# Attention and ELU feed-forward in one kernel: other loads, turns and setup in the first 70 microseconds

## The chip, the cores and the metric

The kernel runs on one core of a Trainium2 chip. The metric is the device time of one execution in microseconds (us). The engines are PE (TensorE, matmuls; PEld is its loading of weights), DVE (VectorE), ACT (ScalarE), POOL (GpSimd) and SP (SyncE, which here only issues DMAs). Each engine works through its own queue in order; waits between queues are semaphores. A DMA issue takes time on the engine that issues it.

## The reference

Causal attention with a window of 128 and a linear bias per head, for 8 batches, 8 heads, 576 positions and a head size of 64, and behind it a feed-forward layer with ELU:

```python
scores = scale * np.matmul(q, k.transpose(0, 1, 3, 2))
...
mask = (rel >= 0) & (rel < window)
scores = np.where(mask, scores + bias[None], -1000000000.0)
...
attn = np.exp(scores)
attn = attn / (np.sum(attn, axis=-1, keepdims=True) + 1e-09)
return np.matmul(attn, v).astype(np.float32)
...
h = x @ w_in
g = np.where(h > 0.0, h, alpha * (np.exp(np.minimum(h, 0.0)) - 1.0))
return (g @ w_out).astype(np.float32)
```

The 8 x 576 rows of x (512 wide) are the attention output of all heads; w_in is 512 x 2048, w_out 2048 x 512. Inputs and output are float32.

## The kernel before

All matmul operands are float16; the loads convert. A batch's positions are cut into 5 blocks (four of 128, one of 64). `BANKS` lists 16 score groups per batch: block 0 in two groups of four heads, blocks 1 to 3 in four groups of two heads, block 4 in two groups of four heads. For a group, `scores(b, s)` multiplies keys by queries into one PSUM bank (four to eight matmuls; for batch 0 four or two more with `cI` and `DM` that add bias and mask) and ACT takes the exponential into `EX`. `cut` (batch 1 on) masks by a minimum on DVE. `values(b, s)` multiplies `EX` by the values `VP`; a column of ones in `VP` gives the sums. `normalize(b, i, half)` divides on DVE (L424, L425) into `xn`; `turn(b, i)` transposes `xn` to `xT` (batches 0 and 1 on PE with a DVE copy, L438 and L440; later ones by a DMA).

The feed-forward part works on blocks t of 512 rows of x, 16 pieces j each. `hidden(t, j)` is 16 matmuls (8 wide ones from t = 2 on) of `w_in_sb` and `xT` into one of three `hp` banks (L461); ACT takes the exponential `e` (L465), POOL clamps it (L466). `elu(t, j)`, one step later, joins both on DVE into `g` (L473). `output(t, j)` is four matmuls of `g` with a quarter of `w_out_sb` (L504); after four of them ACT copies the bank to `ob` (L508) and SP writes it out. For t = 0 piece j uses rows 128*(j//4) on and the w_in columns 512*(j%4) on, so pieces 0 and 4 use the first chunk of `w_in`.

How q and k get to `QK`, heads on the free axis and the 64 head dimensions on partitions: batch 0 by `transposes_half(a, hq, w)`, eight PE transposes (L290) of half a of the positions, four heads, k (w = 1) or q (w = 0), with four copies each (L296; k on ACT, q on DVE); batch 1 by `transposes` (`put` copies first on DVE, then on ACT, both L308); the last 64 positions by `transposes_tail` (L341, DVE copies L346); from batch 2 on by `squares` on DVE and `collect` DMAs. v is loaded into `vs` and copied into `VP` by `place_v`, each copy one set of 32 rows, on DVE (L123), ACT (L125) or POOL (L121).

PSUM has 8 banks: two for scores, transposes and turns (`ps_s`), two for value groups (`ps_v`, `av`), three for `hp` (`ps_h`), one for `op` (`ps_o`).

What runs when is written by hand. `at(s, f, ...)` puts a call into step s, `HID` and `OUT` say which piece of `hidden` and `output` a step holds, `LATER` delays them from given pieces on. A step is emitted in this order: scores; hidden; elu of the step before; `early` calls; `later` calls (values and normalize, then turns); everything else (copies of v, DMA issues, setup); output. Each engine's queue follows that order.

Batch 0 starts with `transposes_half` of the first half of the positions. `warm(n)` issues n idle matmuls of the identity (L536) in the first steps. All loads are issued by POOL, in its queue, between its other work. The setup that the masks of later batches need is done on DVE by `zeros` (L211 to L216), `groups` (L227), `terms` (L241), `last_blocks` (L201), `group_rows` (L252), `bands` (L208) and `k_term` (L270), by `fill_q` on ACT (L261) and `fill_k` on POOL (L265); `fill_other` copies the rows to the other `QK` by DMA.

The steps of before around the change, on PE:

- steps 0 to 4: scores(0, s), eight fillers, values of the group before, from step 4 with hidden(0,0), then hidden(0,1) in step 5;
- steps 6 and 7: values(0,5) and the four `transposes_half` of the second half, then turn(0,1);
- steps 8 to 17: scores(0, 6) to (0, 15), one hidden piece each, values; from step 13 outputs of t = 0;
- steps 18 to 21: the four `transposes` of batch 1; scores(1,0) in step 21.

Of the kernel before, what the change touches and what calls it, by code (L numbers as in the profile page):

```python
# [19 lines left out]
def kernel(  # L20
# [9 lines left out]
    nc = tc.nc  # L30
# [7 lines left out]
    XBAR = 2  # L38
    RING = 3 * S

    LATER = {16: (3, 4), 24: (4, 5), 30: (5, 5), 32: (6, 6), 40: (7, 7)}
    VW = D + 2
    V = nc.vector

# [4 lines left out]
    ps_s = ctx.enter_context(tc.tile_pool(name="ps_s", bufs=2, space=PSUM))  # L49
    ps_v = ctx.enter_context(tc.tile_pool(name="ps_v", bufs=2, space=PSUM))  # L50
    ps_h = ctx.enter_context(tc.tile_pool(name="ps_h", bufs=3, space=PSUM))
    ps_o = ctx.enter_context(tc.tile_pool(name="ps_o", bufs=1, space=PSUM))
# [33 lines left out]
    def load_half(b, w, a, h0=0, h1=H):  # L86
        if b not in stq:
            stq[b] = stage.tile([128, 2, H, 4, D], F16, name="stq")
        nc.gpsimd.dma_start(
            stq[b][64 * a:64 * a + 64, w, h0:h1, :, :].rearrange("p h j d -> p h (j d)"),  # L90
            (q, k)[w][b, h0:h1, 256 * a:256 * a + 256, :].rearrange("h (p j) d -> p h (j d)", j=4))

    def load_v_half(b, a):
        if b not in vs:
            vs[b] = stage.tile([128, H, 4, D], F16, name="vs", tag="vs", bufs=2)
        nc.gpsimd.dma_start(
            vs[b][64 * a:64 * a + 64, :, :, :].rearrange("p h j d -> p h (j d)"),
            v[b, :, 256 * a:256 * a + 256, :].rearrange("h (p j) d -> p h (j d)", j=4))
# [28 lines left out]
    def load_wi(i, n=1):  # L127
        c = slice(512 * i, 512 * i + 512 * n)
        nc.gpsimd.dma_start(w_in_sb[:, :, c], moe_w_in[:, c].rearrange("(c p) f -> p c f", p=128))
# [8 lines left out]
    with tc.manual_schedule():  # L138
# [9 lines left out]
        load_half(0, 0, 0, 4, 8)  # L148
        load_v_half(0, 0)
        load_wi(0)  # L150
        load_wi(1)
        load_half(0, 1, 1)
        load_half(0, 0, 1)
        nc.gpsimd.iota(posi[:, 0:512].rearrange("p (n j i) -> p n j i", j=4, i=32),
                       pattern=[[128, 4], [1, 4], [4, 32]], base=0, channel_multiplier=0)
        nc.gpsimd.iota(posi[:, 512:576], pattern=[[1, 64]], base=512, channel_multiplier=0)
# [295 lines left out]
        def hidden(t, j):  # L452
            w, c0, f0, nf = place(t, j)
            p = hps[t, j] = ps_h.tile([128, 512], F32, name="hp", tag="hp")
            a = (512 * t + c0) % RING
            cuts = [(0, w, a)] if a + w <= RING else [(0, RING - a, a), (RING - a, w, 0)]
            for l in range(nf):
                fc = f0 + l
                for u0, u1, x0 in cuts:
                    for c in range(4):  # L460
                        nc.tensor.matmul(  # L461
                            p[:, l * w + u0:l * w + u1], w_in_sb[:, c, fc * 128:(fc + 1) * 128],
                            xT[:, c, x0:x0 + u1 - u0], start=(c == 0), stop=(c == 3))
            e = es[t, j] = work.tile([128, 512], F32, name="e", tag="e")
            nc.scalar.activation(e, p, AF.Exp)  # L465
            nc.gpsimd.tensor_scalar(out=e, in0=e, scalar1=1.0, scalar2=0.0, op0=ALU.min, op1=ALU.max)  # L466
# [66 lines left out]
        def warm(n):  # L533

            for _ in range(n):
                nc.tensor.matmul(spare[:, 0:128], ident, ident, start=True, stop=True)  # L536
# [4 lines left out]
        def at(s, f, *a):  # L541
            tasks.setdefault(s, []).append((f, a))


        HID, OUT, late = {}, {}, (0, 0)
        first = [0, 1, 4, 5, 2, 6, 3, 7]
        for m in range(16 * NTB):
            late = LATER.get(m, late)
            t, j = divmod(m, 16)
            HID[m + (4 if m < 2 else 6) + late[0]] = t, first[m] if m < 8 else j  # L550
            OUT[13 + m + late[1]] = t, j
        warm(20)
        transposes_half(0, 0, 1, ps_h, "hp")
        warm(8)
# [6 lines left out]
        at(0, place_v, 0, 0, (2,), nc.scalar)  # L561
        at(0, place_v, 0, 0, (3,), nc.gpsimd)
        at(0, place_v, 0, 1, (0, 1, 2), nc.gpsimd)
        at(0, load_v_half, 0, 1)
        at(0, load_wi, 2)
        at(1, scores, 0, 1)
        at(1, warm, 8)
        at(1, place_v, 0, 1, (3,), nc.scalar)
        for i in (2, 3, 4):
            at(i, warm, 8)  # L570

        for b in range(B):
            s0 = 16 * b + (5 if b else 2)
            for s in range(16):
                i, p = BANKS[s]
                half = p if i in (0, 4) else p // 2
                sv = s if b == 0 and s < 6 else s0 + s
                if b or s > 1:
                    at(sv, scores, b, s)
                if b:  # L580
                    at(sv, cut, b, s)
                sv += 2 if b > 2 or b == 2 and s > 1 else 1
                at(sv, values, b, s)
                if i in (0, 4) or p % 2:
                    at(sv, normalize, b, i, half)
                    if half:
                        at(sv + 1, turn, b, i)
            if b == 0:
                for hq in range(2):
                    at(6 + hq, transposes_half, 1, hq, 1, *((ps_h, "hp") if hq else (ps_o, "op")))  # L590
                    at(6 + hq, transposes_half, 1, hq, 0, *((ps_h, "hp") if hq else (ps_s, "sps")))
                at(14, transposes_tail, 0)
            if b + 1 < B:
                for hp in range(NP if b == 0 else 0):
                    at(18 + hp, transposes, 1, hp)
                for n in range(8 if b else 0):
                    at(s0 + (2 + n if b > 1 else (1, 2, 5, 6, 3, 4, 7, 12)[n]), squares, b + 1, n)
                    at(s0 + (6 + n if b > 1 else 8 + n if n < 4 else 9 + n), collect, b + 1, n)
                at(s0 + (24 if b else 31), transposes_tail, b + 1)
            if b + 2 < B and b:  # L600
                for i, w in enumerate((1, 0)):
                    at(s0 + 10 + 3 * i, load_qk, b + 2, w)
                    at(s0 + 26 + i, load_tail, b + 2, w)
                at(s0 + 15, load_v4, b + 2)
                at(s0 + 19, load_v4_tail, b + 2)
                for n in range(4):
                    for u in range(2):
                        at(s0 + 20 + 2 * n + u, place_v, b + 2, n, (2 * u, 2 * u + 1), nc.gpsimd)


        for u in range(2):
            at(6 + u, place_v, 0, 2, (2 * u, 2 * u + 1), nc.gpsimd)
            at(10 + u, place_v, 0, 3, (2 * u, 2 * u + 1), nc.gpsimd)
        at(1, load_wi, 3)
        at(3, load_wo, 0, 1)
        at(8, terms)
        at(5, load_wo, 1, 1)
        at(8, load_wo, 2, 1)
        at(10, load_wo, 3, 1)
        at(3, zeros)  # L620
        at(8, last_blocks)
        at(5, groups)
        at(10, group_rows)
        at(12, bands)
        for n, m in enumerate((12, 15, 18, 23, 26)):
            at(m, fill_q, n)
            at(m, fill_k, n)
        for h in range(H):
            at(12 + h, k_term, h)
        for n in range(5):  # L630
            at((21, 22, 23, 25, 28)[n], fill_other, n)
        for i, w in enumerate((1, 0)):
            at(6 + i, load_tail, 0, w)
            at(12 + i, load_qk, 1, w)
            at(17 + i, load_qk, 2, w)
            at(16 + 5 * i, load_tail, 1, w)
            at(38 + i, load_tail, 2, w)
        at(8, load_v4_tail, 0)
        at(14, load_v4, 1)
        at(22, load_v4_tail, 1)  # L640
        at(20, place_v, 1, 0, (0, 1), V)
        at(21, place_v, 1, 0, (2, 3), V)
# [9 lines left out]

        for s in range(max(OUT) + 1):
            now = tasks.get(s, [])
            early = [x for x in now if x[0] in (cut, transposes_half, transposes, transposes_tail, warm)]
            later = [x for x in now if x[0] in (values, normalize)] + [x for x in now if x[0] is turn]
            for f, a in now:
                if f is scores:
                    f(*a)
            if s in HID:  # L660
                hidden(*HID[s])
            if s - 1 in HID:
                elu(*HID[s - 1])
            for f, a in early + later:
                f(*a)
            for x in now:
                if x not in early and x not in later and x[0] is not scores:
                    x[0](*x[1])
            if s in OUT:
                output(*OUT[s])  # L670
# [30 lines left out]
```

## Time and profile before

| what | value |
|---|---|
| median of five runs | 348.54 us (345.94 to 349.95) |
| the profiled execution, one of the five | 349.95 us |
| its span, first to last instruction | 348.2 us |
| PE busy | 329.1 us, 95% |
| DVE, POOL, ACT busy | 250.1, 213.8, 207.6 us |
| mean granted clock of PE | 0.988 |
| read from and written to memory | 36.70 and 9.44 MB |

The busy shares are averages over the whole span. PE's time holds 143.1 us of output matmuls (L504), 152.2 us of hidden matmuls (L461), 51.0 us of scores (L358) and 7.7 us of the 68 fillers (L536). Where a line of a timeline has square brackets, they hold the engine's idle time before that line and what ended it. In lists of waits the columns are total us, times, longest. In the clock row of the page each digit is one fortieth of the span, in tenths of full speed.

### The profile page before, as it was taken

What the parts mean: (1) busy time and instruction counts of PE and PEld (TensorE: products, weight loads), DVE (VectorE), ACT (ScalarE), POOL (GpSimd) and SP (SyncE); (2) the same over time, 40 slices, a digit from 0 to 9 for tenths busy, and PEclk for the clock granted to TensorE, in tenths of its full rate; (3) what the DMA queues carried; (4) which work ended last, traced back from release to release, by engine and by line L of the source; (5) the groups of instructions that cost most, each with busy time, mean ns of one, the idle gap of its engine ahead of it and who ended that gap; (6) DMA issues with size and microseconds to landing.
All of it is one profiled execution on the core that took longest, in us unless ns stands there. A gap on an engine that the chain in (4) does not pass through costs nothing.

```text
span 348.2 us, 9296 instructions
## 1 busy us (share of the span) xinstructions
PE 329.1 (95%) x3588; PEld 244.1 (70%) x3588; DVE 250.1 (72%) x572; ACT 207.6 (60%) x359; POOL 213.8 (61%) x326
## 2 busy tenths in 40 slices
PE   5979899798989989999999999999999999999995
PEld 4758677477766757777777777777777777766664
DVE  4587788889769679949994999498967676533330
ACT  5564657977875646665656665666566666344431
POOL 8655966654778955995689568947972223333330
PEclk9996999999999999999999999999999999999999
DMA  7999599956992698479968984996462222311122
GB/s 89 188 201 138 77 175 168 195 100 128 141 167 60 112 202 115 108 106 196 110 107 121 196 108 93 146 189 94 105 107 56 54 47 50 70 34 32 30 60 64
DMA packets 66428, 39.54 MB, mean 114 GB/s; under 512 B 31120, under 2 KB 60048, under 8 KB 66384
## 3 DMA queue, kind: packets, MB, share of 16 engines
q0 software_dynamic: 41936, 18.35, 44.6%
q1 hardware_dynamic: 24272, 20.46, 26.7%
q8 instruction: 28, 0.46, 0.5%
q10 hardware_dynamic: 176, 0.13, 0.1%
q14 instruction: 16, 0.13, 0.1%
HBM read 36.70 MB, written 9.44 MB: 133 GB/s over the span
## 4 chain that ended last, share of the span: by engine, by line
PE 79%; DVE 8%; DMA 5%; POOL 3%; ACT 2%; issue 1%; SPq 1%; POOLq 0%; DVEq 0%; ACTq 0%
PE hp L461 32%; PE op L504 30%; PE sp L358 7%; PE av L404 4%; DMA xT<-xn 2%; DMA QK<-tt 2%; PE spare L536 2%; DVE g L473 2%; DVE EX L390 2%; DVE tt L327 2%; PE sp L378 1%; POOL VP L121 1%; DVE xn L425 1%; POOL e L466 1%; ACT e L465 1%
## 5 line engine op out<-in xcount | busy, mean ns | idle before, releaser
L466 POOL TENSOR_SCALAR e<-e 128x512 f32<-128x512 f32 x144 | 90.4, 629 | 113.5 <-ACT e L465 103.7
L461 PE MATMUL hp<-xT,wi 128*128 128x256 f16 (+3 forms) x1536 | 152.2, 248 | 1.2 <-DVE xT L440 0.6
L473 DVE SCALAR_TENSOR_TENSOR g<-e,hp 128x512 f16<-128x512 f32 x144 | 98.0, 681 | 67.8 <-POOL e L466 66.8
L504 PE MATMUL op<-wo,g 128*128 128x512 f16 x560 | 143.1, 379 | 0.6 <-ACT ob L508 0.6
L461 PEld LDWEIGHTS <-wi 128*128 128x128 f16 x1536 | 119.6, 99 | 15.2 <-issue 1.1
L382 ACT ACTIVATE EX<-sp 128x512 f16<-128x512 f32 x128 | 76.6, 598 | 64.8 <-PE sp L358 50.9
L465 ACT ACTIVATE e<-hp 128x512 f32<-128x512 f32 x144 | 86.0, 597 | 48.5 <-PE hp L461 46.7
L121 POOL TENSOR_SCALAR VP<-vs 32x512 f16<-32x512 f16 x106 | 70.2, 662 | 8.7 <-DMA vs<-in_v_dram 1.6
L504 PEld LDWEIGHTS <-g 128*128 128x128 f16 x560 | 47.1, 97 | 35.1 <-issue 0.8
L358 PEld LDWEIGHTS <-QK 128*128 128x128 f16 (+1 forms) x576 | 39.3, 99 | 29.0 <-issue 2.3
L390 DVE TENSOR_TENSOR EX<-EX,band 128x512 f16<-128x512 f16 x112 | 55.2, 493 | 3.2 <-ACT EX L382 2.4
L358 PE MATMUL sp<-QK 128*128 128x128 f16 (+3 forms) x576 | 51.0, 216 | 1.1 <-ACT QK L308 0.9
L404 PE MATMUL av<-VP,EX 128*128 128x65 f16 x576 | 39.0, 194 | 4.9 <-DVE EX L390 4.1
L404 PEld LDWEIGHTS <-EX 128*128 128x128 f16 x576 | 32.0, 98 | 7.9 <-DVE EX L390 4.9
L425 DVE TENSOR_TENSOR xn<-av,rden 128x256 f16<-128x256 f32 x80 | 34.0, 425 | 2.8
L327 DVE STREAM_TRANSPOSE tt<-stq 128x512 f16<-128x512 f16 x48 | 33.7, 701 | 2.5 <-DMA QK<-tt 2.5
L508 ACT COPY ob<-op 128x512 f32<-128x512 f32 x35 | 20.5, 585 | 15.2 <-PE op L504 14.0
L424 DVE RECIPROCAL rden<-av 128x4 f32<-128x4 f32 x80 | 14.0, 175 | 4.4 <-PE av L404 4.1
L536 PE MATMUL spare<-ident 128*128 128x128 f16 x68 | 7.7, 291 | 3.8 <-DVE kmod L169 3.8
L125 ACT COPY VP<-vs 32x512 f16<-32x512 f16 x16 | 9.8, 615 | 0.4
L536 PEld LDWEIGHTS <-ident 128*128 128x128 f16 x68 | 6.5, 135 | 4.1 <-DVE kmod L169 3.8
L378 PE MATMUL sp<-DM,cI 128*128 128x256 f16 (+1 forms) x40 | 7.4, 292 | 0.0
(87 smaller groups left out, 146.0 us busy)
## 6 DMA issues: line engine op xcount, KB each, us to landing
out_dram<-ob SPq DMA_DIRECT2D x126, 64.0 KB, 2.0
QK<-tt SPq DMA_DIRECT2D x48, 128.0 KB, 2.4
stq<-in_k_dram POOLq DMA_DIRECT2D x7, 512.0 KB, 7.0
stq<-in_q_dram POOLq DMA_DIRECT2D x7, 512.0 KB, 7.7
vs<-in_v_dram POOLq DMA_DIRECT2D x7, 512.0 KB, 9.1
wi<-in_moe_w_in_dram POOLq DMA_DIRECT2D x4, 512.0 KB, 10.2
wo<-in_moe_w_out_dram POOLq DMA_DIRECT2D x4, 512.0 KB, 7.2
QK<-QK SPq DMA_DIRECT2D x5, 256.0 KB, 4.6
```

Source lines behind the costliest of these rows:

```text
L121: engine.tensor_scalar(out=o, in0=i, scalar1=1.0, scalar2=0.0, op0=ALU.mult, op1=ALU.add)
L327: V.transpose(out=tt[b][:, dh, w, hs, :, :].rearrange("p h j i -> p (h j) i"), in_=stq[b][:, w, hs, :, 32 * dh:32 * dh + 32].rearrange("p ...
L358: nc.tensor.matmul(t[:, o:o + n], qk[0:r, kc, 1, h, :], qk[0:r, qc, 0, h, 0:n], start=b > 0 or o == 0, stop=b > 0)
L382: nc.scalar.activation(e[:, 0:512], t, AF.Exp, scale=0.125)
L390: V.tensor_tensor(out=e, in0=e, in1=band[:, c:c + n].unsqueeze(1).broadcast_to([128, 512 // n, n]), op=ALU.min)
L404: nc.tensor.matmul(a[:, l, :], e[:, c:c + 128], vp[:, n, h, 0:D + 1], start=st, stop=sp)
L425: V.tensor_tensor(out=xnt[b, i][:, 4 * half:4 * half + 4, :], in0=a[:, :, 0:D], in1=r.unsqueeze(2).broadcast_to([128, 4, D]), op=ALU.mult)
L461: nc.tensor.matmul(p[:, l * w + u0:l * w + u1], w_in_sb[:, c, fc * 128:(fc + 1) * 128], xT[:, c, x0:x0 + u1 - u0], start=(c == 0), stop=(c ...
L465: nc.scalar.activation(e, p, AF.Exp)
L466: nc.gpsimd.tensor_scalar(out=e, in0=e, scalar1=1.0, scalar2=0.0, op0=ALU.min, op1=ALU.max)
L473: V.scalar_tensor_tensor(out=gs[t][:, f0:f0 + nf, c0:c0 + w], in0=sh(es.pop((t, j))), scalar=1.0, in1=sh(hps.pop((t, j))), op0=ALU.subtrac ...
L504: nc.tensor.matmul(ops[t], gs[t][:, fc, ts * 128:(ts + 1) * 128], w_out_sb[:, fc, :], start=(fc == 0), stop=(fc == NFC - 1))
```

## The change

It changes the order of calls; apart from 16 more fillers the computation is the same instructions on the same data, with one copy of v moved from POOL to ACT.

- Loads: the second chunk of `w_in` goes from before the second halves of k and q to after the first copies of v; the second half of v goes to directly behind the second half of q. The third chunk stays behind the second one, the fourth moves from step 1 to 3, the four loads of w_out from steps 3, 5, 8, 10 to 5, 8, 9, 10; the last 64 rows of batch 0 (`load_tail`, `load_v4_tail`) from steps 6, 7, 8 to 13, 14, 16.
- In a step, `transposes_half` and `warm` now come after values, normalize and turn. Fillers stand in steps 2 to 6, two more groups of eight.
- `transposes_half` of the second half: steps 5, 6, 6, 7.
- hidden(0,1) moves from step 5 to 9, behind hidden(0,4) in step 8; the pieces after them and the outputs of t = 0 come one step later, and `LATER` gives the step back for hidden from t = 1 on; the outputs of t = 0 end one step later.
- scores(0,14) and (0,15) move from steps 16 and 17 to 21 and 22, their values, normalize and turn(0,4) with them; `transposes_tail(0)` moves from step 14 to 20; scores(1,0) from step 21 to 22, where scores(1,1) is as well.
- The `transposes` of batch 1 move from steps 18, 19, 20, 21 to 19, 20, 21, 21; `load_qk(1)` from steps 12, 13 to 11, 12.
- Setup: zeros step 3 to 4, groups 5 to 9, terms 8 to 10, last_blocks 8 to 12, group_rows 10 to 13, bands 12 to 14; the first `fill_q` and `fill_k` from 12 and 15 to 14 and 16.

```diff
-    LATER = {16: (3, 4), 24: (4, 5), 30: (5, 5), 32: (6, 6), 40: (7, 7)}
+    LATER = {16: (2, 3), 24: (3, 4), 30: (4, 4), 32: (5, 5), 40: (6, 6)}
...
         load_wi(0)
-        load_wi(1)
         load_half(0, 1, 1)
         load_half(0, 0, 1)
+        load_v_half(0, 1)
...
-        first = [0, 1, 4, 5, 2, 6, 3, 7]
+        first = [0, 4, 1, 5, 2, 6, 3, 7]
...
-            HID[m + (4 if m < 2 else 6) + late[0]] = t, first[m] if m < 8 else j
-            OUT[13 + m + late[1]] = t, j
+            HID[(m + 7 if m else 4) + late[0]] = t, first[m] if m < 8 else j
+            OUT[14 + m + late[1]] = t, j
...
-        at(0, load_v_half, 0, 1)
+        at(0, load_wi, 1)
         at(0, load_wi, 2)
...
-        for i in (2, 3, 4):
+        for i in range(2, 7):
             at(i, warm, 8)
...
-                sv = s if b == 0 and s < 6 else s0 + s
+                sv = s0 + s + ((b, s) == (1, 0) if b else -2 if s < 6 else 5 if s > 13 else 0)
...
-                for hq in range(2):
-                    at(6 + hq, transposes_half, 1, hq, 1, *((ps_h, "hp") if hq else (ps_o, "op")))
-                    at(6 + hq, transposes_half, 1, hq, 0, *((ps_h, "hp") if hq else (ps_s, "sps")))
-                at(14, transposes_tail, 0)
+                for n, (hq, w, pool, tag) in enumerate(((0, 1, ps_h, "hp"), (0, 0, ps_s, "sps"),
+                                                        (1, 1, ps_h, "hp"), (1, 0, ps_h, "hp"))):
+                    at((5, 6, 6, 7)[n], transposes_half, 1, hq, w, pool, tag)
+                at(20, transposes_tail, 0)
...
-                    at(18 + hp, transposes, 1, hp)
+                    at((19, 20, 21, 21)[hp], transposes, 1, hp)
...
+        at(6, place_v, 0, 2, (0, 1), nc.gpsimd)
+        at(7, place_v, 0, 2, (2,), nc.gpsimd)
+        at(7, place_v, 0, 2, (3,), nc.scalar)
         for u in range(2):
-            at(6 + u, place_v, 0, 2, (2 * u, 2 * u + 1), nc.gpsimd)
             at(10 + u, place_v, 0, 3, (2 * u, 2 * u + 1), nc.gpsimd)
...
-        at(3, zeros)
-        at(8, last_blocks)
-        at(5, groups)
-        at(10, group_rows)
-        at(12, bands)
-        for n, m in enumerate((12, 15, 18, 23, 26)):
+        at(4, zeros)
+        at(9, groups)
+        at(10, terms)
+        at(12, last_blocks)
+        at(13, group_rows)
+        at(14, bands)
+        for n, m in enumerate((14, 16, 18, 23, 26)):
...
-            at(12 + h, k_term, h)
+            at(14 + 3 * h // 4, k_term, h)
...
-            early = [x for x in now if x[0] in (cut, transposes_half, transposes, transposes_tail, warm)]
-            later = [x for x in now if x[0] in (values, normalize)] + [x for x in now if x[0] is turn]
+            early = [x for x in now if x[0] in (cut, transposes, transposes_tail)]
+            later = [x for x in now if x[0] in (values, normalize)] + [x for x in now if x[0] is turn] + \
+                [x for x in now if x[0] is transposes_half] + [x for x in now if x[0] is warm]
```

More of the change, by code (lines that the diff above doesn't have):

```diff
@@ L608 @@
                         at(s0 + 20 + 2 * n + u, place_v, b + 2, n, (2 * u, 2 * u + 1), nc.gpsimd)
+        at(6, place_v, 0, 2, (0, 1), nc.gpsimd)
+        at(7, place_v, 0, 2, (2,), nc.gpsimd)
+        at(7, place_v, 0, 2, (3,), nc.scalar)
         for u in range(2):
-            at(6 + u, place_v, 0, 2, (2 * u, 2 * u + 1), nc.gpsimd)
             at(10 + u, place_v, 0, 3, (2 * u, 2 * u + 1), nc.gpsimd)
[L614 to L618, printed above, removed]
-        at(10, load_wo, 3, 1)
-        at(3, zeros)
-        at(8, last_blocks)
-        at(5, groups)
-        at(10, group_rows)
-        at(12, bands)
-        for n, m in enumerate((12, 15, 18, 23, 26)):
+        at(3, load_wi, 3)
+        at(5, load_wo, 0, 1)
+        at(8, load_wo, 1, 1)
+        at(9, load_wo, 2, 1)
+        at(10, load_wo, 3, 1)
+        at(4, zeros)
[5 more added lines that the diff above has]
+        for n, m in enumerate((14, 16, 18, 23, 26)):
             at(m, fill_q, n)
@@ L632 @@
         for i, w in enumerate((1, 0)):
-            at(6 + i, load_tail, 0, w)
-            at(12 + i, load_qk, 1, w)
+            at(13 + i, load_tail, 0, w)
+            at(11 + i, load_qk, 1, w)
             at(17 + i, load_qk, 2, w)
@@ L637 @@
             at(38 + i, load_tail, 2, w)
-        at(8, load_v4_tail, 0)
-        at(14, load_v4, 1)
+        at(16, load_v4_tail, 0)
+        at(15, load_v4, 1)
         at(22, load_v4_tail, 1)
```

## The prediction

> **What bounds the kernel now.** I read the page's engine rows and clock row first, then PE's waits, then the chain and the timelines of the first 70 us, since step 29 on is the same in both kernels.
>
> ```profile
> PE 329.1 (95%) x3588; PEld 244.1 (70%) x3588; DVE 250.1 (72%) x572; ACT 207.6 (60%) x359; POOL 213.8 (61%) x326
> ...
> PEclk9996999999999999999999999999999999999999
> ```
> ```profile
> PE xps L438 <- DVE xn L425: 2.3, 1, 2.3
> PE av L404 <- POOL VP L121: 0.9, 1, 0.9
> PE sp L358 <- ACT QK L308: 0.9, 1, 0.9
> ...
> PE op L504 <- ACT ob L508: 0.6, 1, 0.6
> PE hp L461 <- DVE xT L440: 0.6, 1, 0.6
> ```
> PE is busy 95%: time is won where PE waits or runs slowly. The listed waits lie before 70 us: 2.30 at 22.65 (turn(0,1) waits for `xn`), 0.62 at 25.9, 0.89 at 38.6, and 0.64 + 0.89 + 0.22 + 0.81 in steps 21 to 24. The fourth clock digit is a drop. PE's timeline and the one-stage windows (PE, PEld, DVE, ACT, POOL busy, then granted clock) show its size:
>
> ```profile
> 14.48 1.06 PE L536 MATMUL spare<-ident 128*128 128x128 f16 x8
> ...
> 16.31 0.61 PE L536 MATMUL spare<-ident 128*128 128x128 f16 x8
> ...
> 26.51 1.89 PE L461 MATMUL hp<-xT,wi 128*128 128x128 f16 x16 [0.62 <-DVE xT L440]
> ...
> 34.26 1.06 PE L461 MATMUL hp<-xT,wi 128*128 128x128 f16 x16
> ```
> ```profile
> 26.50:32.90 6.40, 6.39 (x54) 5.47 (x55) 4.36 (x15) 2.19 (x5) 3.92 (x8) 0.50 0.92 117
> ...
> 60.60:64.00 3.40, 1.87 (x16) 0.96 (x15) 2.68 (x5) 3.30 (x7) 1.74 (x4) 1.00 1.11 127
> ```
> After the gap at 22.65 the clock is 0.50 for 6.4 us. In the chain the work from 26.51 to 33.71 takes 7.2 us; at the rates seen later (hidden group 0.89, score group 0.55, value group 0.12) it is 4.2: the drop costs 3.0. Eight fillers take 0.85 to 0.97 until 15.7 us and 0.45 from then on, so PE starts at half speed too. Half speed ended 6.9 us after the last idle moment at the start (8.8 to 15.7) and 6.4 us after it here (26.5 to 32.9). An idle 1.53 us in 3.4 (the last line, PE busy 1.87) brought no drop.
>
> POOL is second in line around step 10. Its timeline gives start-to-start prices: clamp of `e` 0.7, pair of V copies 1.37, w_out load 0.85, tail load 0.78, K or Q load 0.97, `fill_k` 1.1. Below its lines stand one of DVE's timeline and two of ACT's, used further down.
>
> ```profile
> 36.62 0.82 POOL L132 DMA_DIRECT2D wo<-in_moe_w_out_dram  x1
> 37.51 0.60 POOL L466 TENSOR_SCALAR e<-e 128x512 f32<-128x512 f32 x1
> 38.20 1.29 POOL L121 TENSOR_SCALAR VP<-vs 32x512 f16<-32x512 f16 x2
> ...
> 40.27 1.04 POOL L266 TENSOR_SCALAR QK<-TK 32x1024 f16<-32x1024 f16 x1
> 41.37 0.94 POOL L82 DMA_DIRECT2D stq<-in_k_dram  x1
> ```
> ```profile
> 11.65 1.40 DVE L123 COPY VP<-vs 32x512 f16<-32x512 f16 x2
> ```
> ```profile
> 60.62 0.58 ACT L508 COPY ob<-op 128x512 f32<-128x512 f32 x1
> ...
> 62.23 1.01 ACT L308 COPY QK<-tp 64x1024 f16<-64x1024 f16 x1
> ```
>
> **The change, part by part.** I replay each engine's queue in its new order with these durations.
>
> **Loads: nothing.** Second halves of k and q land at 17.5 and 20.0 now, while PE's order reaches them at 21.0. Earlier landing is not used: the new order takes k at about 22. If the cover failed (K 5 us late) PE would wait some 4 us. `wi` chunk 1 is issued at 12.95 instead of 5.7; with its 8 to 12 us it lands by 25, and hidden(0,1) now wants it at 28.
>
> **Start: +2.0.** Values now come before the fillers. values(0,0) needs the V copies, which DVE ends at 13.05 (the L123 line); PE gets there at 12.53, so 0.57 idle where fillers stood. Behind it in PE's order are fillers and scores(0,2), 14.25 instead of 13.60. If the two rows above hold, an idle moment restarts the count, and full speed comes 6.4 to 6.9 us after 13.1, at 19.8 instead of 15.7. 4.1 us at half speed cost 2.0. Bounds: 0 (so short a wait restarts nothing; 1.5 us idle at 60.6 took nothing) and 2.0. I take 2.0, since both returns of the clock followed 6.4 us without a gap.
>
> The Trainium skill ("TensorE: Matmul & The Clock Gate", Part 1: The HAM clock gate) says that a free-running window of about 3.4 us, busy throughout, is enough. By it, full speed would come between 16.5 and 19.9, and this term would be an estimated 1.3, the sum 351.5; the trace's 6.4 and 6.9 us need two windows. The same page (Part 4: PE-mode transpose) says transposes do not count as busy; no row here isolates that, and it would speak for a still later return.
>
> **Fillers: +0.9.** Two more groups of eight, in steps 5 and 6, 0.45 each.
>
> **Steps 5 to 8: -4.0.** `zeros` (L213 to L216, 1.65 on DVE) moves behind normalize(0,1,0), so elu(0,0) and normalize(0,1,1) come late: 1.65 + 0.7 + 0.6 after 21.9 gives `xn` at 24.9; PE is there at 24.25 and waits 0.7. Then L296's four copies (1.2) hold scores(0,6) to 26.15, 0.65 more; xT is copied at 26.55. With the 0.57 that is 1.9 of waits for 2.9 now, and none of one piece: the 3.0 of the drop go. hidden(0,4) starts at 26.8, and at the end of hidden(0,2) PE stands at 32.6 where the kernel before, with the same work done, stands at 34.2: 1.6 ahead.
>
> **Steps 10 to 18 on POOL: the gain is held there.** Both tail loads (1.56), the V tail (0.8) and the memsets (0.24) are now in this stretch: POOL's steps are 3.14, 3.02, 1.65, 1.46, 2.56, 1.68, 3.36, 1.65, 2.75, together 21.3 (18.8 before). PE's own work there is 17.4, since scores and values of the last rows are gone (20.8 before). So POOL, not PE, sets the pace: from e(0,5) at 31.6 to 52.9, and e(0,12) is ready at 53.5. DVE, in order, does elu(0,12) to 54.25 and only then the tail copies (L346, 0.85). scores(0,14), which PE reaches at about 54.5, needs these: 55.15. If the clamp were not late, that wait would be gone. The work of `terms`, `last_blocks` and `group_rows` (2.0, 1.7, 2.2 on DVE) I cost at nothing: it is spread over steps 10, 12 and 13, where elu waits for POOL anyway; without that cover each would delay an elu by its length.
>
> **Steps 21 to 24: +3.4 to here.** Score tiles, transposes and turns share two PSUM buffers (`ps_s`). Four transposes tiles and scores(0,14), (0,15), (1,0), (1,1) now come together. Each transposes tile is freed by DVE 0.68, then ACT 1.01 (L308); each score tile by its exponential, 0.60. ACT's queue is: put(1,1), V copy, EX(0,14), e(0,14), put(1,2), put(1,3), V copy, `ob` (to 62.0), EX(0,15). So scores(0,15) starts at 59.8, scores(1,0) at 60.85, scores(1,1) only at 62.65. Then three value tiles need the two `av` buffers: values(1,1) waits for normalize(0,4,1) until 67.25. hidden(1,0) starts at 70.75; it was 69.01. From step 11 that is 38.1 us for 34.8.
>
> **Steps 25 to 33: +0.45.** Outputs are one step behind, so 0.86 of PE work comes later, into step 29. Waits of 0.42 (at 81.2) and 0.75 (at 83.9) lie there and can take it up: between 0 and 0.86 is left, and I take the middle.
>
> Sum: 70.75 - 69.0 + 0.45 = +2.2 on the profiled execution, 349.95 us (348.2 span and 1.75 around it): **352.2 us**. The profiled run is the highest of the five, 1.4 above the median of 348.54. I take nothing off for that: part of the spread is likely whether the gap at 22.65 brings the drop, and this gap is gone.
>
> **Rivals.**
> - *Full speed on time* (0.57 idle restarts nothing): the start term falls away, 350.2. For it: 0.22 to 1.5 us waits later in the trace bring no drop. Against it: clock up only after 6.4 us without a gap, twice.
> - *A second drop.* In the replay PE is busy about a third of 59.4 to 62.8, and idle 1.85 of the 3.4 after it. The drop at 26 followed 2.9 idle in 3.9; 1.53 in 3.4 brought none. If it comes it costs up to the 3.0 of now: 355.2. It decides if the score waits of step 22 add up to over 2 us.
> - *Faster: POOL does not hold PE back.* If POOL's steps 10 to 18 take no longer than PE's 17.4 (its DMA issues cheaper, or e(0,5) earlier) and the clock comes on time, PE is 3.6 ahead at step 11, loses the 0.89 wait for V copies at 38.6, keeps both, and the last rows, taken out of the full steps, save half of the 2.56 of waits in steps 21 to 24: -5.8 + 0.45, **344.6**. For it: POOL idles some 8 us between 29 and 57 now. Against it: it idles because PE is slow there.
> - *The load order does nothing at all*: included above, at no price.
>
> **How the numbers follow.** Forecast 0.42 (it stands at the 1% bound, 352.0: 0.28 above, 0.14 below), second drop 0.16, on time 0.22, faster 0.20 (0.17 over 1%). Faster 0.17, same 0.39, slower 0.44. 1% is about what a measurement of this kernel can tell from no change, five runs spreading over 4 us. The forecast's own range is 350.2 to 353.5; over the cases 346 to 356.5.
>
> **What would show it.** Right: PE idle about 0.6 at 12.5; filler groups at 0.85 or more until 19 us; no clock digit under 9 at 26 to 33; POOL without idle from 31 to 53; scores(0,14) waiting for L346; PE waits on L308, L382 and L425 of over 4 us between 55 and 70. Wrong: POOL idling for ACT in steps 12 to 18, fillers at 0.45 by 16 us, hidden(1,0) before 66 us, or a clock of 0.50 near 60.

## The result and the profile after

The changed kernel takes 351.57 us (median of 28 runs, 349.79 to 355.39), the kernel before 348.54 (49 runs, 345.94 to 351.26). The ratio is 1.010, with a 95% interval of 1.0076 to 1.0123: about 1% slower. The profiled execution of after is one of its slowest, 355.35 us with a span of 353.6; its part from 124 us on stands for some executions only.

Engine and clock row of the page of after:

```profile
PE 331.6 (94%) x3604; PEld 245.0 (69%) x3604; DVE 250.9 (71%) x572; ACT 207.9 (59%) x360; POOL 212.7 (60%) x325
...
PEclk9999999999999989999999999999999999999998
```

The low digit near 30 us is gone; there is one of 8 at about 130 us instead. From PE's waits of after (total us, times, longest):

```profile
PE hp L461 <- DVE g L473: 2.8, 4, 1.2
...
PE av L404 <- DVE rden L424: 1.5, 1, 1.5
PE sp L358 <- ACT EX L382: 1.4, 1, 1.4
```

The 2.30 for `xn` and the 0.89 for POOL's copies of v are no longer there, and 0.89 for L308 has become 0.2. In their place PE waits for `elu` (L473) between 35 and 46 us (2.46 of the 2.8; the fourth wait, of 0.36, is at 163 us, where before has it too), and for score and value banks in steps 21 to 24. PE's timeline of after, at the places that the prediction names:

```profile
12.69 0.38 PE L404 MATMUL av<-VP,EX 128*128 128x65 f16 x4 [0.16 <-DVE VP L123]
...
17.59 1.06 PE L536 MATMUL spare<-ident 128*128 128x128 f16 x8
...
19.53 1.46 PE L461 MATMUL hp<-xT,wi 128*128 128x128 f16 x16
...
26.23 1.06 PE L461 MATMUL hp<-xT,wi 128*128 128x128 f16 x16
...
43.40 1.05 PE L461 MATMUL hp<-xT,wi 128*128 128x128 f16 x16 [1.15 <-DVE g L473]
...
55.29 0.40 PE L358 MATMUL sp<-QK 64*128 64x64 f16 x8
...
62.48 0.38 PE L358 MATMUL sp<-QK 128*128 128x128 f16 x4 [1.36 <-ACT EX L382]
...
66.97 0.29 PE L404 MATMUL av<-VP,EX 128*128 128x65 f16 x4 [1.51 <-DVE rden L424]
...
70.39 1.06 PE L461 MATMUL hp<-xT,wi 128*128 128x128 f16 x16
...
126.45 0.29 PE L404 MATMUL av<-VP,EX 128*128 128x65 f16 x4 [1.47 <-DVE EX L390]
...
129.49 1.81 PE L461 MATMUL hp<-xT,wi 128*128 128x256 f16 x8 [1.66 <-DMA xT<-xn]
```

Fillers run at half speed until past 17.59, and hidden(0,0), at 19.53, is partly slow; hidden(0,4), at 26.23, is at full speed; hidden(1,0) comes at 70.39, 1.38 later than before (69.01). The eighth `ob` copy is 1.69 later (121.28 for 119.59). Of the 5.4 us between the two spans, the rest appears from 124 us on: two waits, and behind them eight wide matmuls in 1.81 us where they else take 1.04.

The stretch in which the prediction saw POOL at its limit, as one window (us busy of PE, PEld, DVE, ACT, POOL, then granted clock), before and after:

```profile
31.00:53.00 22.00, 21.11 (x288) 16.27 (x287) 15.83 (x36) 12.80 (x21) 15.87 (x22) 0.96 0.96 131
```
```profile
31.00:53.00 22.00, 18.86 (x243) 14.23 (x242) 21.22 (x50) 12.52 (x20) 19.58 (x28) 1.00 1.32 168
```

DVE is busy 21.22 of 22 us, 96%; POOL 19.58, with four waits of 0.31 to 0.42 between. DVE has 14 instructions more there, and single ones are longer. DVE's timeline, before and then after, for the first operation of `terms` and for one of `last_blocks`:

```profile
26.77 0.46 DVE L244 TENSOR_SCALAR pm<-posi 32x576 f32<-32x576 int32 x1
...
28.76 0.25 DVE L178 TENSOR_SCALAR nd<-posi,rowf 128x64 f32<-128x64 int32 x1
```
```profile
32.62 0.90 DVE L244 TENSOR_SCALAR pm<-posi 32x576 f32<-32x576 int32 x1
...
36.97 0.67 DVE L178 TENSOR_SCALAR nd<-posi,rowf 128x64 f32<-128x64 int32 x1
```

0.46 became 0.90 and 0.25 became 0.67, in a stretch where POOL is at work nearly without pause.

### The profile page after: what moved, and what is told of

The parts are those of the page before. It is cut to its first block, busy times and chain, and to the rows that moved or that the text cites. A ratio compares the mean times of both kernels' runs of the same rounds, so it can differ in the third digit from the quotient of the medians.

```text
span 353.6 us, 9328 instructions
## 1 busy us (share of the span) xinstructions
PE 331.6 (94%) x3604; PEld 245.0 (69%) x3604; DVE 250.9 (71%) x572; ACT 207.9 (59%) x360; POOL 212.7 (60%) x325
## 4 chain that ended last, share of the span: by engine, by line
PE 74%; DVE 14%; DMA 5%; ACT 3%; POOL 1%; issue 1%; SPq 1%; POOLq 0%; ACTq 0%; DVEq 0%
PE hp L461 30%; PE op L504 29%; PE sp L358 6%; PE av L404 4%; DVE g L473 3%; DMA xT<-xn 3%; DMA QK<-tt 2%; PE spare L536 2%; DVE EX L390 2%; DVE tt L327 2%; DVE xn L425 2%; ACT EX L382 1%; PE sp L378 1%; DVE QK L296 1%; SPq L510 1%
## 5 line engine op out<-in xcount | busy, mean ns | idle before, releaser
L473 DVE SCALAR_TENSOR_TENSOR g<-e,hp 128x512 f16<-128x512 f32 x144 | 98.0, 681 | 66.0 <-POOL e L466 64.9
L121 POOL TENSOR_SCALAR VP<-vs 32x512 f16<-32x512 f16 x105 | 69.3, 660 | 8.9 <-DMA vs<-in_v_dram 1.7
L536 PE MATMUL spare<-ident 128*128 128x128 f16 x84 | 9.4, 286 | 3.8 <-DVE kmod L169 3.8
L536 PEld LDWEIGHTS <-ident 128*128 128x128 f16 x84 | 7.5, 132 | 4.1 <-DVE kmod L169 3.8
```

Source lines behind the costliest of these rows:

```text
L121: engine.tensor_scalar(out=o, in0=i, scalar1=1.0, scalar2=0.0, op0=ALU.mult, op1=ALU.add)
L473: V.scalar_tensor_tensor(out=gs[t][:, f0:f0 + nf, c0:c0 + w], in0=sh(es.pop((t, j))), scalar=1.0, in1=sh(hps.pop((t, j))), op0=ALU.subtrac ...
```

## The experiments

Unless a text says otherwise, an edit is to the changed kernel. Ratios are to the kernel before, with a 95% interval. The kernel before had medians of 349.11, 349.22 and 349.19 us in the three sessions, so its times here lie half a microsecond above the first ones.

**after_again**: the changed kernel, unaltered.

> The changed kernel once more, for a second profile. Theory: the start is the same (half speed of PE until about 20 us, the first group of hidden(1,0) at 70.4, 1.4 us later than before), and the 3.5 us that the first profile lost between 124 and 134 us (a wait of 1.66 for a transposing DMA, then three microseconds at half speed) is an event of some executions only: without it the span is near 349.5 to 350.5. Rival: that loss belongs to the change and comes in every run, span 353 to 354. Median of the times 350.5 to 352.

352.33 us (6 runs), 1.012 [1.006, 1.018]. hidden(1,0) at 70.81. The score waits of step 22 are those of after (0.19 and 1.37), but the clock dropped behind them this time, and again at 130 us. PE's timeline and a one-stage window of after_again:

```profile
61.27 1.90 PE L461 MATMUL hp<-xT,wi 128*128 128x128 f16 x16
```
```profile
61.00:66.00 5.00, 4.61 (x48) 3.53 (x47) 2.65 (x6) 2.90 (x6) 1.52 (x3) 0.66 0.89 175
```

The same waits bring a drop in one execution and none in another. Among the profiles below it is the rule rather than the exception: of the eight with the later last rows, five show a clock under 0.9 between 55 and 65 us (after_again, fillers_first, setup_early, loads_back, loads_back_again); of the six without them none does.

**fillers_first**: the fillers of steps 1 to 3 stand ahead of the values again.

```diff
-            early = [x for x in now if x[0] in (cut, transposes, transposes_tail)]
+            early = [x for x in now if x[0] in (cut, transposes, transposes_tail) or x[0] is warm and 0 < s < 4]
...
-                [x for x in now if x[0] is transposes_half] + [x for x in now if x[0] is warm]
+                [x for x in now if x[0] is transposes_half] + [x for x in now if x[0] is warm and not 0 < s < 4]
```

> The changed kernel with the fillers of steps 1 to 3 put back ahead of values. Theory (the idle moment at 12.5 us restarts the count to full speed): PE does not idle there, eight fillers take 0.45 from 15.7 us on, the first hidden group starts 1.6 to 2.0 us earlier (17.6 to 18.0 instead of 19.5), and the time falls by about 2 us, ratio to the changed kernel 0.994. Rival (full speed depends on when the execution started, not on the idle moment): full speed still comes near 20 us and the time does not change by more than 0.5 us. Second rival: the clock comes early but DVE, which is busy 96 percent from 34 to 52 us, takes the gain back: first hidden group 2 us earlier, hidden(1,0) less than 0.7 us earlier.

350.56 us (12), 1.009 [1.004, 1.013]: 1.0 below the changed kernel by the medians, 0.6 by the means (351.64 for 352.28). The two intervals overlap, so even that is not clear of noise. Its profiled execution refutes the prediction's rule for the start. PE's timeline of fillers_first:

```profile
9.60 0.62 PE L536 MATMUL spare<-ident 128*128 128x128 f16 x8
...
12.12 0.29 PE L404 MATMUL av<-VP,EX 128*128 128x65 f16 x4 [0.62 <-DVE VP L123]
```

Full speed was there by 9.6 us, 5.8 us behind PE's first matmul at 3.8, and 0.62 idle at 12.1 did not end it.

**last_rows_back**: scores(0,14) and (0,15), their loads, `transposes_tail(0)`, the `transposes` of batch 1 and scores(1,0) in the steps of before; `last_blocks` one step earlier.

```diff
-                sv = s0 + s + ((b, s) == (1, 0) if b else -2 if s < 6 else 5 if s > 13 else 0)
+                sv = s0 + s + (0 if b else -2 if s < 6 else 0)
...
-                at(20, transposes_tail, 0)
+                at(14, transposes_tail, 0)
...
-                    at((19, 20, 21, 21)[hp], transposes, 1, hp)
+                    at(18 + hp, transposes, 1, hp)
...
-        at(12, last_blocks)
+        at(11, last_blocks)
...
-            at(13 + i, load_tail, 0, w)
+            at(6 + i, load_tail, 0, w)
-        at(16, load_v4_tail, 0)
+        at(8, load_v4_tail, 0)
```

> The changed kernel with the last rows of batch 0 scored in steps 16 and 17 again (with their loads, their transposes and the transposes of batch 1 in the steps of the kernel before); everything else stays changed. Theory (the pile-up on the two score banks in steps 21 to 24 costs 2 us and more than it saves before): PE waits between 55 and 70 us fall from 4.5 to about 2.5, and hidden(1,0) starts 1 to 2 us earlier, about 68.7 to 69.4. Rival (POOL and DVE hold the stretch from 31 to 53 us anyway, so taking the last rows out of it is what pays): steps 14 to 18 get longer by the 2 us of work that returns and hidden(1,0) is not earlier than 70.4.

351.35 us by the median, but the 12 runs lie in 346.64 to 352.73, their mean is 350.44, and the ratio is 1.003 [0.998, 1.007]. The profile is clear where the times are not: waits between 55 and 70 us sum to 2.2 instead of 4.1, and hidden(1,0) stands 49.0 us behind hidden(0,0) instead of 50.9. In that execution a wait of 1.37 for `xn` at 37 brought a drop there, which took some of it back.

**before_filled**: the kernel before, with 34 more fillers in its gap at 22.65 us.

```diff
+        def warm_gap(n):
+            t = ps_o.tile([128, DO], F32, name="spare2", tag="op")
+            for _ in range(n):
+                nc.tensor.matmul(t[:, 0:128], ident, ident, start=True, stop=True)
...
+        at(7, warm_gap, 34)
...
-            early = [x for x in now if x[0] in (cut, transposes_half, transposes, transposes_tail, warm)]
+            early = [x for x in now if x[0] in (cut, transposes_half, transposes, transposes_tail, warm, warm_gap)]
```

> The kernel before with 34 more fillers between its transposes of the second half and turn(0,1), where PE idles for 2.3 us at 22.65. Nothing is done earlier: the wait for xn stays, it is only filled. Theory (the gap costs 2.3 us itself and a further 3.0 by the drop to half speed): no half speed between 26 and 33 us, and the time is 2 to 3 us below before, ratio 0.992 to 0.994. Rival (DVE and POOL hold that stretch, the half speed is hidden behind them): the clock stays up and the time moves by less than 1 us. The executions of before that take 346 to 347 us would then be those in which the gap brings no drop, and this kernel's times should lie with them.

347.74 us (12), 0.998 [0.994, 1.001]. All runs have a mean granted clock of 0.998 or more (0.9904 in the kernel before, and none of its 85 runs in the three sessions above 0.995). PE's timeline of before_filled:

```profile
22.96 2.06 PE L542 MATMUL spare<-ident 128*128 128x128 f16 x34 [1.15 <-ACT QK L296]
...
27.32 1.05 PE L461 MATMUL hp<-xT,wi 128*128 128x128 f16 x16 [0.76 <-DVE xT L440]
```

hidden(0,4) takes 1.05 instead of 1.89, and from there hidden(1,0) is 39.45 us off instead of 42.50: the drop's price is 3.05 in these two profiles, for 3.0 forecast. hidden(0,4) starts 0.8 later, which leaves 2.2; the runs show 0.8 (by the ratio, whose interval reaches 1) to 1.4 (by the medians) of it. The times still spread over 345.57 to 349.59 with no drop in any, so the drop does not make the whole spread of before. It makes part of it: of the 85 runs of before, the 23 with a mean clock of 0.995 average 347.3 us, the 19 with 0.988 average 349.6.

**setup_early**: `groups`, `terms` and `zeros` in steps 1, 2 and 3, `last_blocks` in 8, `group_rows` in 11.

```diff
-        at(4, zeros)
-        at(9, groups)
-        at(10, terms)
-        at(12, last_blocks)
-        at(13, group_rows)
+        at(3, zeros)
+        at(1, groups)
+        at(2, terms)
+        at(8, last_blocks)
+        at(11, group_rows)
```

> The changed kernel with the mask setup earlier on DVE: groups in step 1, terms in step 2, zeros in step 3, last_blocks in step 8, group_rows in step 11. Theory (not POOL but DVE holds the stretch from 34 to 52 us, where it is busy 96 percent and PE waits 2.5 us for elu's g and 0.6 for xn): these waits fall under 1 us together, POOL idles more between its clamps, hidden(1,0) starts about 48.5 us after hidden(0,0) instead of 50.9, and the time falls by 2 to 2.5 us, ratio to the changed kernel about 0.994. Rival (the prediction's: POOL's queue sets the pace of steps 10 to 18): POOL stays without idle there, hidden(1,0) comes less than 0.7 us earlier and the time stays within 0.7 us.

351.91 us (12), 1.007 [1.003, 1.011]. The window of setup_early:

```profile
31.00:53.00 22.00, 20.13 (x267) 15.50 (x264) 15.52 (x36) 13.68 (x20) 20.40 (x29) 1.00 1.38 185
```

DVE falls from 21.22 to 15.52, and POOL, at 20.40 of 22, is then the busier one. Counted from hidden(0,0), hidden(0,13) is 3.5 us earlier than in after, scores(0,14) 1.9, hidden(1,0) only 0.3 (50.6 for 50.9): a wait of 1.06 for L308, one of 0.82 for copies of v and a drop at 61 us took the rest. In the times the gain is not clear of noise: the ratio's interval overlaps that of the changed kernel.

**both_back**: the edits of fillers_first and last_rows_back together.

> The changed kernel with both parts undone that were undone singly: fillers ahead of values in steps 1 to 3, last rows of batch 0 in steps 16 and 17. Theory (the two losses add up, about 1 and 2 us of mean): 349 to 349.5, ratio to before between 0.999 and 1.003. Rival (they share one loss, since the later clock and the pile-up wait for the same engines): not below 350, no better than the last rows undone alone.

348.50 us (14), 0.997 [0.993, 1.000]: no slower than before. With its profiled execution the start is settled in one more respect. PE's timeline of both_back, and one of its windows:

```profile
8.82 0.58 PE L358 MATMUL sp<-QK 64*128 64x128 f16 x4 [0.25 <-DVE QK L296]
...
16.63 1.06 PE L536 MATMUL spare<-ident 128*128 128x128 f16 x8
...
19.21 1.42 PE L461 MATMUL hp<-xT,wi 128*128 128x128 f16 x16
```
```profile
9.00:19.00 10.00, 10.00 (x89) 7.85 (x88) 3.97 (x13) 4.71 (x9) 4.80 (x7) 1.00 1.32 183
```

PE had no idle after 8.82 and stayed at half speed until about 20. No idle moment can have restarted a count. The record shows a granted clock of 1.00 in that stretch all the same: it does not show the slow start, the matmuls' durations do.

**all_three**: both_back with the setup of setup_early.

> Both parts undone and the mask setup early as well (groups step 1, terms 2, zeros 3, last_blocks 8, group_rows 11). Theory (DVE is what is left in the way between 31 and 45 us, its lateness makes the 1.4 us wait for xn and a drop of the clock at 38): 346 to 347.5, ratio to before 0.992 to 0.996. Rival (DVE work early delays normalize and turn of the first rows as much as it helps later): 348.5 to 350, no gain over both undone.

347.22 us (12), 0.995 [0.992, 0.998]. This is the version that beats both kernels, the one before by half a per cent. hidden(1,0) is 45.3 us behind hidden(0,0); 48.1 in both_back, 50.9 in after, 51.2 in before. In these profiles the earlier setup is worth 2.8 on this way without the pile-up of steps 21 to 24, and 0.3 with it; in the times it is 1.3 by the medians (348.50 to 347.22), with overlapping intervals.

**loads_back**: chunk 1 of w_in ahead of the second halves of k and q, second half of v behind the first copies, as before.

```diff
+        load_wi(1)
...
-        load_v_half(0, 1)
...
-        at(0, load_wi, 1)
+        at(0, load_v_half, 0, 1)
```

> The changed kernel with the order of loads of the kernel before: second chunk of w_in ahead of the second halves of k and q, second half of v behind the first copies of v. Theory (the prediction's: the order of loads is worth nothing, since PE reaches the second halves at 22 us): within 0.6 us of the changed kernel, no wait on a DMA in PE's list, and k and q land 2 to 3 us later. Rival: PE reaches the second halves before they land when the clock comes early, and waits for up to 2 us in those executions; mean 0.5 to 1 us slower than the changed kernel.

354.57 us (6), 1.0145 [1.009, 1.020]. Full speed came at about 8 us in the profiled execution, PE was early, and its waits have two that no other profile has:

```profile
PE thp L290 <- DMA stq<-in_k_dram: 1.1, 1, 1.1
...
PE tsps L290 <- DMA stq<-in_q_dram: 0.5, 1, 0.5
```

A drop followed (clock 0.59 from 20 to 25 us). **loads_back_again** is the same kernel once more, to see whether that is the rule:

> The changed kernel with the loads in their former order once more, for more times of it. Theory now (the profile showed PE waiting 1.07 us for the second half of k and 0.49 for q in an execution whose clock came before 9 us, and the clock falling after it): a loss in those executions alone, median 0.5 to 2 us above the changed kernel, and in a profile with full speed only from 16 to 20 us no wait on a DMA. Rival (the order is worth nothing, the six times were drawn high): median 351.5 to 352.5, as the changed kernel.

352.07 us (12), 1.008 [1.004, 1.011], mean 352.62 for 352.28 of the changed kernel. Again full speed came by 8.6 us, but there were no waits for loads. All 18 runs together average 353.1, 0.8 above the changed kernel. That is not clear of noise, so the order of the loads is worth between nothing and about one us, in favour of the new one; the cover of the old order is thin.

**last_rows_alone**: the kernel before, with the later last rows as its only change (the reverse of last_rows_back, less `last_blocks`).

> The kernel before with one part of the change alone: scores(0,14) and (0,15), their values and turn in steps 21 and 22, scores(1,0) in step 22, transposes_tail in step 20, the transposes of batch 1 in steps 19, 20, 21, 21, the loads of the last rows in steps 13, 14, 16. Theory (the pile-up on the two score banks in steps 21 to 24 is the larger loss of the change): PE waits for L382, L308 and L424 of over 3.5 us between 55 and 72 us, time 1.5 to 2.5 us above before, ratio 1.004 to 1.007. Rival (the pile-up costs only because DVE and POOL arrive late in the changed kernel): within 0.7 us of before.

351.55 us (10), 1.008 [1.005, 1.012]. This part alone makes nearly the whole difference between before and after. PE's timeline of last_rows_alone:

```profile
60.18 0.61 PE L316 MATMUL tp<-ident,stq 128*128 128x128 f16 x8 [1.14 <-ACT EX L382]
...
63.88 0.38 PE L358 MATMUL sp<-QK 128*128 128x128 f16 x4 [0.88 <-ACT EX L382]
...
66.98 0.30 PE L404 MATMUL av<-VP,EX 128*128 128x65 f16 x4 [1.15 <-DVE xn L425]
...
68.55 0.29 PE L404 MATMUL av<-VP,EX 128*128 128x65 f16 x4 [1.26 <-DVE rden L424]
```

These four make 4.4 us; with 0.40 and 0.19 the waits from 55 to 72 come to 5.0, for 2.56 in steps 21 to 24 of before.

**fewer_fillers**: the groups of fillers of steps 5 and 6 are left out.

```diff
-        for i in range(2, 7):
+        for i in range(2, 5):
```

> The changed kernel without the two added groups of fillers (steps 5 and 6). Theory (they stand on PE's path and cost 0.45 each): 0.5 to 0.9 us faster than the changed kernel; hidden(0,4) starts 7.0 to 6.3 us after hidden(0,0) instead of 6.7, if the wait for xn does not take it up. Rival (they fill time in which PE would wait for normalize and the copies of q anyway): the waits for xn and for L296 grow by the 0.9 and the time stays within 0.4 us.

352.48 us (6), 1.011 [1.006, 1.016]: nothing won. Waits for `xn` (0.6) and for `EX` (0.3) took the place of the 0.9 of fillers, and in the profiled execution the clock dropped at 25.5.

**best**: all_three with the copies of the fourth block of v of batch 0 two steps earlier, two loads of w_out one step later, and one group of fillers less.

```diff
-        for i in range(2, 7):
+        for i in range(2, 6):
...
-            at(10 + u, place_v, 0, 3, (2 * u, 2 * u + 1), nc.gpsimd)
+            at(8 + u, place_v, 0, 3, (2 * u, 2 * u + 1), nc.gpsimd)
...
-        at(9, load_wo, 2, 1)
-        at(10, load_wo, 3, 1)
+        at(10, load_wo, 2, 1)
+        at(11, load_wo, 3, 1)
```

> All three (fillers first, last rows early, setup early) and the last copies of v in steps 8 and 9 instead of 10 and 11, with two w_out loads a step later, and the fillers of step 6 left out. Theory (PE's wait of 1.3 us for these copies at 34 us is what POOL's queue still costs): the wait is gone, 345.5 to 347, ratio to before 0.989 to 0.994. Rival (POOL's queue only moves its lateness to the clamps of e): the wait for g or for xT grows instead, 346.8 to 347.6, no gain over all three.

347.75 us (12), 0.998 [0.995, 1.001]; not better than all_three. The wait for copies of v (1.3) went; one of 1.60 for `xn` at 37.3 came.

## Why the prediction was right, and where it was not

The time was right: 352.2 forecast, 351.57 measured. It was so in part by luck. The forecast adds 2.2 to 349.95, the slowest of five runs; from median to median the change costs 3.0. The base was 1.4 too high and the sum 0.8 too low, and within the sum errors of either sign cancel: fillers and start were priced too high, drops that come back elsewhere at nothing. (The terms of the headings add up to +2.75, and -1.1 to the end of hidden(0,2) where the replay has -1.6; the forecast goes by the replay.) In the two profiles the places agree: 2.3 ahead there for 1.6 forecast, 1.38 late at hidden(1,0) for 1.75. Term by term:

- *Loads: nothing.* Not contradicted: 0.8 over 18 runs, not clear of noise. The price if the cover fails was put at 4; waits of 1.1 and 0.5 were seen once, with a drop behind them.
- *Start, +2.0.* The mechanism is refuted. That full speed came at about 20 us in the profile of after, as forecast (19.8), and hidden(0,0) 1.74 later than before, is luck: it came at about 17 in after_again, the same kernel. An idle moment restarts no count: both_back had none after 8.8 and was at half speed until 20, fillers_first had one of 0.62 and kept full speed. The idle was 0.16 in after and 0.49 in after_again, for 0.57, since DVE's copies took 0.89 instead of 1.40. By fillers_first the order of the fillers is worth 1.0 at most in the medians, and perhaps nothing. When full speed comes varies between executions, and what decides it stays open. The Trainium skill ("TensorE: Matmul & The Clock Gate", Part 1: The HAM clock gate) says that the same kernel's cold stretch differs by execution, since the window is free-running. The runs agree that it differs (about 20 us in after, 17 in after_again); none shows the window. It also gives about 3.4 us of sustained work as enough; the gapless 10 us of both_back at half speed contradict that figure.
- *Fillers, +0.9.* Mis-sized: about 0. They stand where PE would have waited (fewer_fillers).
- *Steps 5 to 8, -4.0.* Right in kind: no drop at 26, hidden(0,4) at 26.23 (26.8 forecast), end of hidden(0,2) at 32.0 (32.6). Waits were about 0.6 rather than 1.9. The 3.0 for the drop is confirmed by the 3.05 of the profile of before_filled. What the forecast missed is that drops come back elsewhere: the mean granted clock of all runs rose only from 0.9904 to 0.9939. As an estimate, time times the missing share of the clock is 3.4 us per execution of before, 2.1 of after and 0.1 of before_filled. So the change kept 1.2 of the 3.0 forecast.
- *Steps 10 to 18, POOL sets the pace.* The sum came out, scores(0,14) at 55.29 for 55.15, by luck: the cause was wrong. DVE was the engine without idle; setup "at nothing" was the mistake. It made elu, and so `g`, late: 2.46 us of waits for L473. Some of its operations were up to 0.4 longer than before, which is not the main thing: in fewer_fillers L244 and L178 took 0.46 and 0.25 again, and PE still waited 1.3 for L473. With the setup gone (setup_early) POOL does take over, at 93%, so the forecast's POOL bound seems to lie just behind.
- *Steps 21 to 24, +3.4.* Right in mechanism and place. Forecast for scores(0,15), (1,0), (1,1), the last values and hidden(1,0): 59.8, 60.85, 62.65, 67.25, 70.75. Measured: 59.82, 60.74, 62.48, 66.97, 70.39. Waits between 55 and 70 were 4.1, over 4 as forecast. Shown by last_rows_back (2.2) and last_rows_alone (ratio 1.008 from this part alone).
- *Steps 25 to 33, +0.45.* hidden(1,0) to the eighth `ob` is 50.89 for 50.58: +0.31.
- *Part of the spread of before is whether the gap brings the drop.* None of 85 runs of before has the full clock, so it is how much of it, not whether; and with no drop at all (before_filled) the times still spread over 4 us. That this rest comes from the start is likely, but argued only.

The rivals. *Full speed on time* would have given 350.2; the median of fillers_first, whose one profile shows full speed even earlier, is near that, 350.56. *A second drop* does occur, in after_again at 61 and in after at 130, but not from the point that the prediction gave: the score waits of step 22 are 1.55 and 1.56 us, under its 2, and behind them only after_again dropped. With five of eight profiles it is part of the changed kernel's usual cost, where the prediction gave it a chance of 0.16 as a case of its own; in after_again hidden(1,0) is 1.4 us further behind hidden(0,0) than in after. The drop at 130 goes with one wait: in the five profiles with it (after, after_again, last_rows_back, both_back, all_three) PE waited 1.1 to 1.8 us for the DMA of `xT`, in the other nine 0.5 or less. Whether that wait is the cause was not tried. *Faster* failed twice over: DVE held PE back, and moving the last rows saved no waits in steps 21 to 24, it added 2.4 in last_rows_alone.

So the change is a gain (no drop at 26) and two losses (the pile-up on the two score banks; setup in DVE's busiest stretch). Undoing these two, with the fillers of steps 1 to 3 ahead of the values again, gives 0.995 (all_three). The pile-up is shown by the times; the setup by the profiles, and by the times only together with the rest.

## What to carry to other kernels

When work is moved out of a full stretch, count the users of the buffers where it arrives: here four transposes and four score groups on two banks cost more (ratio 1.008, last_rows_alone) than the rest of the change brought. Before a move of setup is put at no cost, add up the busy time of its engine, with its neighbours' too, in the new window. A throttle drop that is removed at one gap is worth its price only if the later gaps do not bring one back, so look at the mean clock of many runs as well as at one profile.

## What was not expected of the hardware

- The time of full speed after the start lay between about 8 and 20 us in 14 profiles whose starts are nearly the same, with no relation to idle moments that they show; hidden(0,0) then starts at 15.60 to 19.80. The granted clock reads 1.00 during it.
- DVE's setup operations took 0.46 to 0.90, 0.25 to 0.67 and 0.29 to 0.64 us (L244, L178, L189) when they fell among POOL's work. L244 in setup_early, with POOL idle, took 0.46 again. L189 took 0.74 there, beside a clamp. In after POOL was copying v during L244 and issuing loads during L178 and L189; in fewer_fillers L178 took 0.25 beside the same issue, so what decides it stays open. The Trainium skill ("SBUF — State Buffer", SBUF: two separate sides) calls the port pair that POOL shares with some kinds of DVE operation an exclusive lock, held for a whole instruction. No run isolates it here.
